# Four second-quarter f-tiles as seven-product blocks, with the sums that feed the down projection rearranged around them

## The chip, the cores and the metric

The kernel runs on one core of a Trainium2 chip. The metric is the device time of one launch in microseconds (us). The median before was 258.68 us in three runs (258.34 to 258.99), and 258.51 in four runs once the changed kernel was timed beside it. Most executions lie within 0.3% of the median, which is 0.8 us here. A verdict of faster or slower needs 2%.

Names: PE is TensorE's matmuls, PEld its weight loads, DVE is VectorE, ACT is ScalarE, POOL is GpSimd, and SPq is SyncE's queue, which issues most of the DMAs.

## The reference

```python
x = A_x                                            # 1 x 2048 x 640, bf16
g = sigmoid((x * gate_w).sum(-1, keepdims=True))
a = linear_attention(x, wqkv, H=32) @ wo           # phi(q), phi(k), kv and z per head
b = (gelu(x @ w_gate) * (x @ w_up)) @ w_down       # F = 1728 = 13 * 128 + 64
return g * a + (1 - g) * b
```

The attention output joins the down projection: its q rows, divided by their denominators, and a matrix M = kv @ wo are appended to h and w_down as further contraction rows.

## The kernel before: the parts that matter

The 2048 tokens are worked in four quarters of 512. For each quarter, stage E makes the h rows: for each f-tile of 128 rows it computes gate and up products, a gelu on ScalarE, and one product on VectorE that writes the row (`e_out`). Stage F is the down projection. The order is E(0), all q and k, the kv product, then E(1) F(0) E(2) F(1) E(3) F(2) F(3).

A plain f-tile is ten matmuls of 128x512:

```python
def phase_E(q, ft):                                         # cut
    psg = ps_tile(); e_mm(psg, wg, ft, q)        # 5 x (128x512)
    psu = ps_tile(); e_mm(psu, wu, ft, q)        # 5 x (128x512)
    e_out(q, ft, psg, psu)                       # gelu on ACT, product on DVE
```

A block makes the same f-tile by the Strassen-Winograd scheme: seven products of halves where the plain tile needs eight. It needs sums of weights (`sw_`, made once in the first quarter and stored in HBM), sums of tokens (`tx`), and sums of PSUM banks on the way:

```python
def unit_b(q, ft, fetch):
    ...
    def p5(): two(ub[:, hi_h], s_(1), tx[0], True)          # two(): 2 matmuls of 128x256
    def p1():
        two(ub[:, lo_h], wg[:, 0:2, fs], X[:, 0:2, lo_h])
        nc.scalar.copy(out=gb[:, lo_h], in_=ub[:, lo_h])
        nc.scalar.copy(out=cp, in_=ub[:, hi_h])
    def p6():
        two(ub[:, lo_h], s_(2), tx[1])
        nc.vector.tensor_tensor(out=gb[:, hi_h], in0=ub[:, lo_h], in1=cp, op=ALU.add)
    def p7(): ...                                           # 2 matmuls, an ACT copy
    def p3():
        nc.vector.tensor_tensor(out=ub[:, hi_h], in0=ub[:, hi_h], in1=c3, op=ALU.add)
        ...                                                 # 2 matmuls, read of a later block's sums
    def g5(): mm(gb, wg[:, 4, fs], X[:, 4, :])              # 128x512
    ...                                                     # p2: gelu; u5: 128x512; p4: e_out
    return [p5, p1], [p6], [p7, p3, g5, p2], [u5, p4]       # interleaved with three neighbours
```

Quarters 0, 2 and 3 use blocks. Quarter 1 does not:

```python
runs = {0: blocks([3], 12, range(4, 12), [NF - 1]),
        1: list(range(1, NF)),                              # plain tiles
        2: blocks([NF - 1, 12], 0, range(1, 12), [None]), ...}
```

Stage F uses the same scheme with S sums (of h and q rows) and T sums (of w_down and M), four each, in parts "h" (six k-tiles), "p" (two) and "x" (one). It works in two halves, `a`. All S and T sums of the first F were made on VectorE, nearly all of them during E(1), by the table `side`, which lists what is issued beside each step:

```python
side = {(1, 4): [(s3_tile,), (h_twin, 0), (phase_T, "h", (1,))],
        (1, 5): [(phase_T, "h", (3, 2))],
        (1, 6): [(phase_S, 0, "h", None, (3, 4)), (phase_T, "x", (1, 3))],
        ...                                                 # T p, S p, S x, more of T
        ("F", 0, 0): [(x_tiles,), (t_sums, 2), ...],        # token sums of quarter 2
        ("D", 0, 0): [(den_inv, 4), (den_mul, 6, 7)], ...}

def phase_F(q):                                             # cut
    for a in range(2):
        beside("F", q, a)
        x = ps_tile()                    # 2nd half: x's bank is b11's of the first half
        product(x, ...);  flush()        # flush: matmuls left over from E's last block
        beside("C", q, a)
        product(b11, ...)                # 9 matmuls of 128x320 each
        product(x, S2, T2); product(b22, S1, T1); join(d, b22)
        beside("D", q, a)
        product(x, S3, T3); product(b12, S4, ...)
        halves(...); join(o[0], b11)     # not a: this join reads b11's bank out
        join(o[0], b12); join(o[1], b22)
        product(b21, ..., T4); join(o[1], b21)
```

`join` is VectorE. `t_sums` makes the four token sums of a quarter, `den_mul`, `den_sum`, `den_rec`, `den_inv2` and `den_out` divide the q rows (POOL, DVE, POOL, DVE, POOL), and `pool_hold` copies one element on GpSimd to make that engine wait for a tile. Of the other names in these tables, those ending in `tiles` or `tile` only set up buffers, `h_twin` copies the last, half f-tile, `m_part` makes parts of M, and `w_fetch` reads weight sums from HBM.

## Time and profile before

| | before |
|---|---|
| time, median | 258.51 us |
| span of the profiled run | 256.9 us |
| PE busy | 251.3 us (98%) |
| E(1), counted from the kv product, and the first F | 29.52 + 17.87 = 47.39 us |

From the page of the kernel before, parts 1 and 4: busy us and share of the span of each engine with its number of instructions, then the chain of work that ended last, by engine.

```profile
PE 251.3 (98%) x1725; PEld 161.3 (63%) x1746; DVE 178.4 (69%) x343; ACT 118.8 (46%) x271; POOL 132.8 (52%) x154
PE 98%; issue 0%; DVE 0%
```

TensorE is the limit, and nothing else is on the chain. The next view is the busy time by stretches, E(1) from the kv product on and then the first F. Columns: the stretch, its length, then busy time and number of instructions for each engine, the granted clock, DMA share and GB/s.

```profile
core 0: us, PE busy (x) PEld busy (x) DVE busy (x) ACT busy (x) POOL busy (x), PEclk, DMA share, GB/s
98.07:127.59 29.52, 29.36 (x202) 13.76 (x205) 24.35 (x41) 12.44 (x27) 12.57 (x12) 1.00 0.34 99
127.59:145.46 17.87, 17.87 (x135) 12.55 (x134) 13.61 (x26) 4.37 (x8) 11.65 (x13) 1.00 0.29 82
```

PE has no gap in F and next to none in E; the clock is full. VectorE is 82% busy in E without being on the chain. I count E from the kv product because the first f-tile's first matmul has no record in several traces.

PE's timeline of the kernel before, around the first F's second half. Columns: start, busy us, engine, line, operation, output<-inputs, shapes, count, and in brackets idle time and what ended it, where PE waited.

```profile
135.67 0.99 PE L811 MATMUL banks<-hb,hT_148 128*128 128x320 f16 x6
136.50 0.57 PE L811 MATMUL banks<-hb,pqT_1266 128*128 128x320 f16 x3
136.90 0.98 PE L811 MATMUL banks<-wd,hT_148 128*128 128x320 bf16 x6
```

Read starts, not durations. Three 128x320 matmuls are shown as 0.57 us, but the next group starts 0.40 us later, because matmuls overlap. From start to start a 128x320 matmul takes 0.136 us and a 128x512 one 0.216. The line at 136.90 is the first product of the second half, and its bank was freed in time by VectorE (timeline of VectorE, kernel before):

```profile
135.53 0.55 DVE L713 RECIPROCAL rg<-dtmp 128x64 f32<-128x64 f32 x1 [0.42 <-POOL dtmp L706]
136.00 0.45 DVE L837 SCALAR_TENSOR_TENSOR o_out<-banks,omg_s,sw 128x320 bf16<-128x320 f32 x1
```

The join ends at 136.45, 0.45 us before PE uses the bank.

Blocks already run in the third quarter. Two lines of PE's timeline there, kernel before, are the same step of two successive blocks:

```profile
156.53 0.60 PE L316 MATMUL banks<-xT_90,wg 128*128 128x512 bf16 x3
158.49 0.60 PE L316 MATMUL banks<-xT_90,wg 128*128 128x512 bf16 x3
```

A block takes 1.96 us. A plain tile takes 10 x 0.216 = 2.16 us.

### The profile page before, as it was taken

How to read it: one execution, taken by the hardware profiler on the slowest of the kernel's cores; microseconds unless marked ns; L12 is line 12 of the kernel's file. 1: busy time of each engine (PE TensorE's matmuls, PEld its weight loads, DVE VectorE, ACT ScalarE, POOL GpSimd, SP SyncE). 2: the span in 40 equal slices, each digit the busy share in tenths (PEclk: the TensorE clock that was granted, in tenths of full speed). 3: DMA queues.
4: the chain of work that ended last, by engine and by line, in shares of the span. 5: the costliest groups of instructions: out<-in, count | busy, mean ns of one | idle time of the engine just before them, and what ended most of it. 6: DMA issues, size and time to landing. Idle time of an engine off the chain costs nothing.

```text
span 256.9 us, 4833 instructions
## 1 busy us (share of the span) xinstructions
PE 251.3 (98%) x1725; PEld 161.3 (63%) x1746; DVE 178.4 (69%) x343; ACT 118.8 (46%) x271; POOL 132.8 (52%) x154
## 2 busy tenths in 40 slices
PE   8999999999999999999999999999999999999994
PEld 3555786555556775444476668777666786767672
DVE  0567577788779997679997448884655887278632
ACT  2387676655554234732231168862126875311110
POOL 5005999355540003770048898992879999600000
PEclk9999999999999999999999999999999999999999
DMA  7999999500000019115031554442105710211011
GB/s 223 306 342 350 378 337 312 226 3 0 0 1 3 1 44 310 57 60 121 2 125 51 100 177 144 123 148 51 54 20 125 209 47 0 46 58 56 0 51 51
DMA packets 36361, 30.26 MB, mean 118 GB/s; under 512 B 13938, under 2 KB 34546, under 8 KB 36338
## 3 DMA queue, kind: packets, MB, share of 16 engines
q1 hardware_dynamic: 35618, 29.24, 37.5%
q10 hardware_dynamic: 720, 0.72, 0.9%
q8 instruction: 13, 0.21, 0.4%
q14 instruction: 10, 0.08, 0.1%
HBM read 21.01 MB, written 5.51 MB: 103 GB/s over the span
## 4 chain that ended last, share of the span: by engine, by line
PE 98%; issue 0%; DVE 0%
PE banks L811 27%; PE banks L316 23%; PE banks L406 17%; PE banks L228 14%; PE banks L326 6%; PE banks L528 6%; PE banks L518 2%; PE banks L203 1%; PE banks L818 1%; PE banks L659 0%; PE banks L628 0%; DVE o_out L837 0%; PE banks L598 0%
## 5 line engine op out<-in xcount | busy, mean ns | idle before, releaser
L233 ACT ACTIVATE gl<-banks 128x512 bf16<-128x512 f32 x52 | 31.0, 599 | 28.4 <-PE banks L228 17.1
L425 ACT ACTIVATE phi<-banks 128x512 bf16<-128x512 f32 (+1 forms) x36 | 18.7, 526 | 15.4 <-POOL hold L783 6.8
L238 DVE SCALAR_TENSOR_TENSOR hT_148<-banks,gl 128x512 bf16<-128x512 f32 x26 | 17.9, 691 | 9.0 <-PE banks L316 5.2
L238 DVE SCALAR_TENSOR_TENSOR hb<-banks,gl 128x512 bf16<-128x512 f32 x26 | 17.7, 682 | 8.5 <-PE banks L316 2.6
L833 ACT ACTIVATE m_all<-banks,omg_s 128x320 f32<-128x320 f32 x16 | 8.4, 527 | 31.6 <-PE banks L811 31.6
L783 POOL CAST hold<-phi 128x1 f32<-128x1 bf16 x13 | 2.4, 183 | 38.1 <-DVE phi L427 20.2
L316 PEld LDWEIGHTS <-wg 128*128 128x128 bf16 x150 | 14.7, 98 | 5.5
L380 DVE TENSOR_TENSOR banks<-banks,zacc 128x256 f32<-128x256 f32 x30 | 12.8, 427 | 6.0 <-ACT zacc L377 4.6
L228 PE MATMUL banks<-xT_89,wu 128*128 128x512 bf16 x63 | 16.0, 379 | 0.1
L837 DVE SCALAR_TENSOR_TENSOR o_out<-banks,omg_s,m_all 128x320 bf16<-128x320 f32 x24 | 12.4, 546 | 5.2 <-PE banks L811 5.2
L228 PE MATMUL banks<-xT_89,wg 128*128 128x512 bf16 x63 | 15.7, 379 | 0.1
L837 DVE SCALAR_TENSOR_TENSOR m_all<-banks,omg_s,m_all 128x320 f32<-128x320 f32 x8 | 4.4, 550 | 15.2 <-PE banks L811 15.1
L377 ACT COPY zacc<-banks 128x256 f32<-128x256 f32 x30 | 11.1, 371 | 7.1 <-PE banks L316 7.1
L316 PE MATMUL banks<-tx,wr 128*128 128x256 f16 x76 | 14.0, 273 | 0.0
L228 PEld LDWEIGHTS <-wu 128*128 128x128 bf16 x80 | 7.8, 98 | 9.4 <-DMA wu<-in_B_w_up_dram 0.3
L833 ACT ACTIVATE sw<-banks,omg_s 128x320 f32<-128x320 f32 x8 | 4.2, 527 | 19.6 <-PE banks L811 19.6
L228 PEld LDWEIGHTS <-wg 128*128 128x128 bf16 x80 | 7.5, 98 | 8.6 <-issue 0.5
L406 PE MATMUL banks<-wqk,xT_88 128*128 128x512 bf16 (+2 forms) x78 | 12.7, 321 | 0.1
L691 POOL TENSOR_TENSOR prod<-pq_92,zrep 128x640 f32<-128x640 bf16 x2 | 2.8, 1406 | 18.6 <-DVE kvt L635 18.6
L368 ACT COPY banks<-banks 128x256 f32<-128x256 f32 x30 | 10.7, 357 | 3.0 <-PE banks L316 0.4
L316 PEld LDWEIGHTS <-wu 128*128 128x128 bf16 x90 | 8.8, 98 | 4.6
L406 PE MATMUL banks<-wqk,xT_89 128*128 128x512 bf16 (+1 forms) x59 | 11.6, 343 | 0.1
(282 smaller groups left out, 671.1 us busy)
## 6 DMA issues: line engine op xcount, KB each, us to landing
wr<-stash SPq DMA_DIRECT2D x24, 128.0 KB, 2.2
x_all<-in_A_x_dram SPq DMA_DIRECT2D x4, 640.0 KB, 11.1
out_dram<-o_out SPq DMA_DIRECT2D x15, 160.0 KB, 1.9
wd<-in_B_w_down_dram SPq DMA_DIRECT2D x1, 2080.0 KB, 10.6
wr_1668<-stash SPq DMA_DIRECT2D x16, 128.0 KB, 2.5
wqk<-in_A_wqkv_dram SPq DMA_DIRECT2D x1, 800.0 KB
wg<-in_B_w_gate_dram SPq DMA_DIRECT2D x1, 800.0 KB
wu<-in_B_w_up_dram SPq DMA_DIRECT2D x1, 800.0 KB
```

The source lines that it names most:

```text
L228: nc.tensor.matmul(ps[:, t0 : t0 + tw], lhsT=w[:, dk, ft * P : (ft + 1) * P], rhs=xT[q][:, dk, t0 : t0 + tw], start=(dk == 0), stop=(dk == ...
L233: nc.scalar.activation(out=gl[:], in_=psg[:], func=ACT.Gelu_apprx_tanh)
L238: nc.vector.scalar_tensor_tensor(out=hT_cur[q][:, ft, :], in0=psu[:], scalar=HS, in1=gl[:], op0=ALU.mult, op1=ALU.mult)
L316: nc.tensor.matmul(out, lhsT=lhsT, rhs=rhs, start=start, stop=True, skip_group_check=True)
L326: return lambda: nc.tensor.matmul(ps, lhsT=w[:, k, f * P : (f + 1) * P], rhs=xT[q][:, k, :], start=(k == 0), stop=(k == ND - 1))
L380: nc.vector.tensor_tensor(out=ub[:, hi_h], in0=ub[:, hi_h], in1=c3, op=ALU.add)
L406: nc.tensor.matmul(ps[:, 0 : hi - lo], lhsT=xT[q][:, dk, sl * P : (sl + 1) * P], rhs=wqk[:, dk, lo:hi], start=(dk == 0), stop=(dk == ND - 1),)
L425: nc.scalar.activation(out=e[:, lo:top], in_=ps[:, lo:top], func=ACT.Exp)
L528: nc.tensor.matmul(bank[:, 0:HALF], lhsT=lhsT, rhs=rhs, start=(start and n == 0), stop=(stop and n == NG2 - 1), skip_group_check=True)
L811: nc.tensor.matmul(bank[:, 0:HALF], lhsT=lhs(sa, ia, ka * KS + kk, a), rhs=rhs(sb, kb * KS + kk, jb), start=(start and kk == 0), stop=(sto ...
L833: nc.scalar.activation(out=c[:], in_=bank[:, 0:HALF], func=ACT.Copy, scale=omg[i])
L837: nc.vector.scalar_tensor_tensor(out=out, in0=bank[:, 0:HALF], scalar=omg[i], in1=c[:], op0=ALU.mult, op1=ALU.add)
```

## The change

The intent is to give the second quarter four blocks (f-tiles 8 to 11). Their weight sums are read from HBM into h rows that are written only later and into the S4 tile. Their token sums lie where T4 will be. So S4 and T4, and for VectorE's sake also the third and fourth sums of p and x, move into the first F, and the first and second sums of p and x go to GpSimd. The read of w_down is split in two, so T sums can start earlier. The diff, cut to its core:

```diff
-    def x_tiles():
+    def x_tiles(tx=None):
...
+    WB = range(8, 12)
     runs = {
-        1: list(range(1, NF)),
+        1: blocks([7], 12, WB, [NF - 1]),
...
+    def early_blocks():                  # weight sums into h rows 8..11 and into S4's tile
+        rows = [hb[:, f * QW : (f + 2) * QW].bitcast(FP16) for f in (8, 10)]
+        rows += [SS["4"].rearrange("p k n -> p (k n)")[:, i * WS * P : (i + 1) * WS * P] for i in range(2)]
+        for ft, row in zip(WB, rows):
+            dma(out=row, in_=stash[WF.index(ft)])
...
-        (1, 1): [(m_part, 0), (t_tiles,), (den_mul, 0, 1, 2, 3)],
-        ...                              # S and T sums of (1, 4) to (1, 10), all on VectorE
+        ("S", 0): [(s_tiles, 0), (phase_S, 0, "h", None, (1,)), (x_early,), (t_sums, 1)],
+        ("P", 1): [(m_part, 0), (t_tiles,), (den_mul, 0), (phase_T, "h", (1,)), (hold, lambda: TS[1]),
+                   (den_mul, 1, 2), (den_sum, 0, 0)],
+        ...
+        ("P", 3): [(den_sum, 2, 0), (den_out, 0), (den_sum, 2, 1), (den_rec, 2), (phase_T, "h", (2,)),
+                   (hold, lambda: TS[2]), (den_out, 1), (den_inv2, 2)],
+        ("P", 4): [(s3_tile,), (h_twin, 0)],
+        ("P", 5): [(phase_S, 0, "h", None, (3,)), (hold, lambda: SS[0, 3]), (den_out, 2, 3)],
+        ("P", 6): [(den_mul, 4, 5)] + [(phase_T, part, which, nc.gpsimd) ...]       # p, x: 1, 2
+        + [(phase_S, 0, part, None, (1, 2), nc.gpsimd) for part in "px"],
+        ("C", 0, 0): [(phase_T, "p", (3,)), (phase_T, "x", (3,)), (phase_S, 0, "p", None, (3, 4)),
+                      (phase_S, 0, "x", None, (3, 4)), (phase_S, 0, "h", None, (4,))]
+        + [(phase_T, part, (4,)) for part in "hpx"],
+        ("D", 0, 0): [(t_sums, 2), (lambda: pool_hold(ew["tx"][3][:, 0, 0:1]),), (den_mul, 6, 7), (den_inv2, 4)],
...
+        early_blocks()
+        for ft in range(1, WB[0] - 1):   # f-tiles 1 to 6 stay plain, with fixed banks for 5 and 6
+            if ft > WB[0] - 4:
+                bank_at[0] = 6 if ft == WB[0] - 3 else 4
+            phase_E(1, ft)
+            beside("P", ft)
```

More of the change, by code (lines that the diff above doesn't have):

```diff
@@ L129 @@
     ew = {}
-    def x_tiles():
-        tx = big.tile([P, 10 * HT], FP16, name="tx", tag="pq", bufs=NQ)
+    def x_tiles(tx=None):
+        tx = big.tile([P, 10 * HT], FP16, name="tx", tag="pq", bufs=NQ) if tx is None else tx
         ew["tx"] = [tx[:, 2 * HT * n : 2 * HT * (n + 1)].rearrange("p (k c) -> p k c", k=2) for n in range(4)]
@@ L194, in load_down @@
         wd = ov.tile([P, NF, D], BF16, name="wd", tag="slab_d")
-        dma(out=wd[:, 0 : NF - 1, :], in_=B_w_down[0:FM, :].rearrange("(k p) n -> p k n", p=P))
+        wd_v = B_w_down[0:FM, :].rearrange("(k p) n -> p k n", p=P)
+        for lo, hi in ((0, KH), (KH, NF - 1)):
+            dma(out=wd[:, lo:hi, :], in_=wd_v[:, lo:hi, :])
         for lo in (0, FL):
@@ L748, in ktile, with phase_T @@
         return ktiles(part, k, first, second)[:, kk - PART[part][0], :]
-    def phase_T(part, which=(1, 2, 3, 4)):
+    def phase_T(part, which=(1, 2, 3, 4), eng=nc.vector):
         lo, hi = PART[part]
@@ L758, in phase_T @@
             a0, a1 = {1: ((0, 1), (0, 0)), 2: ((1, 1), 1), 3: ((1, 1), (0, 1)), 4: ((1, 0), 2)}[i]
-            sums(t[i], blk(*a0), blk(*a1) if i in (1, 3) else t[a1], ALU.subtract)
+            sums(t[i], blk(*a0), blk(*a1) if i in (1, 3) else t[a1], ALU.subtract, eng)
     SS = {}
@@ L906, in run_E @@
     def run_E(q):
-        if q == 1:
-            for n, ft in enumerate(runs[q]):
-                phase_E(q, ft)
-                beside(q, n + 1)
-            return
         pipe, plain, at = [], {}, []
@@ L988, with x_early @@
     TS[4] = hb[:, NF * QW : NF * QW + KS * HALF].bitcast(FP16).rearrange("p (k n) -> p k n", n=HALF)
+    def x_early():
+        x_tiles(hb[:, NF * QW : NF * QW + 10 * HT].bitcast(FP16))
+    def early_blocks():
+        rows = [hb[:, f * QW : (f + 2) * QW].bitcast(FP16) for f in (8, 10)]
+        rows += [SS["4"].rearrange("p k n -> p (k n)")[:, i * WS * P : (i + 1) * WS * P] for i in range(2)]
+        for ft, row in zip(WB, rows):
+            row = row.rearrange("p (s c) -> p s c", c=P)
+            dma(out=row, in_=stash[WF.index(ft)])
+            ew["at"][1, ft] = split(row)
     hT_cur[2] = hT0
@@ L1014, in m_part, with hold @@
         phase_M(((0, 0), (0, 1), (1, 0)) if i == 0 else ((1, 1), (2, 0), (2, 1)))
+    def hold(of):
+        pool_hold(of()[:, 0, 0:1])
     def s_pool(q, a, parts="hpx"):
@@ L1019 @@
     side.update({
-        ("S", 0): [(s_tiles, 0), (phase_S, 0, "h", None, (1,))],
-        ("S", 1): [(phase_S, 0, "h", None, (2,))],
-        (1, 1): [(m_part, 0), (t_tiles,), (den_mul, 0, 1, 2, 3)],
-        (1, 2): [(m_part, 1), (den_inv, 0), (den_out, 0, 1)],
-        (1, 3): [(den_inv, 2), (den_out, 2, 3)],
-        (1, 4): [(s3_tile,), (h_twin, 0), (phase_T, "h", (1,))],
-        (1, 5): [(phase_T, "h", (3, 2))],
-        (1, 6): [(phase_S, 0, "h", None, (3, 4)), (phase_T, "x", (1, 3))],
@@ L1028 @@
-        (1, 7): [(phase_T, "h", (4,)), (phase_T, "x", (2, 4))],
-        (1, 8): [(phase_T, "p", (1, 2, 3, 4))],
-        (1, 9): [(phase_S, 0, "p")],
-        (1, 10): [(phase_S, 0, "x")],
-        (1, 12): [(lambda: pool_hold(SS[0, 4][:, KS - 1, 0:1]),), (den_mul, 4, 5)],
-        ("F", 0, 0): [(x_tiles,), (t_sums, 2), (w_fetch, (2, 1), (2, 2), (2, 3))],
-        ("D", 0, 0): [(den_inv, 4), (den_mul, 6, 7)],
-        ("F", 0, 1): [(h_twin, 1), (den_sum, 6, 0), (den_sum, 6, 1), (den_rec, 6), (den_out, 4, 5)],
+        ("S", 0): [(s_tiles, 0), (phase_S, 0, "h", None, (1,)), (x_early,), (t_sums, 1)],
@@ new lines @@
+        ("P", 0): [(phase_S, 0, "h", None, (2,)), (hold, lambda: SS[0, 2])],
+        ("P", 1): [(m_part, 0), (t_tiles,), (den_mul, 0), (phase_T, "h", (1,)), (hold, lambda: TS[1]),
+                   (den_mul, 1, 2), (den_sum, 0, 0)],
+        ("P", 2): [(m_part, 1), (den_sum, 0, 1), (den_rec, 0), (phase_T, "h", (3,)), (hold, lambda: TS[3]),
+                   (den_mul, 3), (den_inv2, 0)],
+        ("P", 3): [(den_sum, 2, 0), (den_out, 0), (den_sum, 2, 1), (den_rec, 2), (phase_T, "h", (2,)),
+                   (hold, lambda: TS[2]), (den_out, 1), (den_inv2, 2)],
@@ new lines @@
+        ("P", 4): [(s3_tile,), (h_twin, 0)],
+        ("P", 5): [(phase_S, 0, "h", None, (3,)), (hold, lambda: SS[0, 3]), (den_out, 2, 3)],
+        ("P", 6): [(den_mul, 4, 5)] + [(phase_T, part, which, nc.gpsimd) for part, which in (("p", (1, 2)), ("x", (1, 2)))]
+        + [(phase_S, 0, part, None, (1, 2), nc.gpsimd) for part in "px"],
+        (1, 6): [(den_rec, 4)],
+        ("F", 0, 0): [(x_tiles,), (w_fetch, (2, 1), (2, 2), (2, 3))],
+        ("C", 0, 0): [(phase_T, "p", (3,)), (phase_T, "x", (3,)), (phase_S, 0, "p", None, (3, 4)),
+                      (phase_S, 0, "x", None, (3, 4)), (phase_S, 0, "h", None, (4,))]
@@ L1036 @@
+        + [(phase_T, part, (4,)) for part in "hpx"],
+        ("D", 0, 0): [(t_sums, 2), (lambda: pool_hold(ew["tx"][3][:, 0, 0:1]),), (den_mul, 6, 7), (den_inv2, 4)],
+        ("F", 0, 1): [(h_twin, 1), (den_out, 4, 5), (den_sum, 6, 0), (den_sum, 6, 1), (den_rec, 6)],
         ("D", 0, 1): [(den_inv2, 6), (den_out, 6, 7)],
@@ L1055 @@
     })
-    for q, st in ((2, 8), (3, 14)):
+    for q, st in ((1, 4), (2, 8), (3, 14)):
         for n in range(4):
-            side[q, 3 + n] = [(den_sum, st, n // 2, slice(H // 2 * (n % 2), H // 2 * (n % 2 + 1)))]
+            side[q, (3 if q > 1 else 2) + n] = [(den_sum, st, n // 2, slice(H // 2 * (n % 2), H // 2 * (n % 2 + 1)))]
     with tc.manual_schedule():
@@ L1064 @@
         phase_KV()
+        early_blocks()
         phase_Zrep()
+        beside("P", 0)
+        for ft in range(1, WB[0] - 1):
[3 more added lines that the diff above has]
+            beside("P", ft)
         for q in range(1, NQ):
```

## The prediction

> **What bounds it now.** TensorE. The page gives PE 251.3 us busy of a 256.9 us span (98%); the chain of waits is PE for 98% of it. The table by stretches gives PE 21.48 of 21.59 us in the plain f-tiles of the second quarter (104.9 to 126.5) and 18.95 of 18.95 in the first F (126.5 to 145.5). No gap there can be won; only fewer streamed columns shorten it. VectorE has 19.64 and 14.69 us in these stretches: off the chain, with little room.
>
> **On PE.** A plain f-tile is ten 128x512 matmuls; in the timeline it repeats every 2.16 us. A seven-product block is fourteen 128x256 and two 128x512: 4608 columns for 5120. In the third quarter, where blocks already run, it repeats every 1.96 us. That is 0.20 us a tile, not 10% (0.216): the six more matmuls cost a little each. The Trainium skill ("TensorE: Matmul & The Clock Gate", "Wait — 56ns, not 53.3ns?") gives about 2.5 ns per matmul beyond its columns; the trace agrees (14 x 109 + 2 x 216 ns = 1.96 us). Four tiles: 0.79 us, all on the chain.
>
> **Added and moved elsewhere.**
> - ScalarE: 12 copies of 0.36 to 0.38 us; it was busy 8.4 of 21.6 us there, so free.
> - VectorE: 8 sums of banks (0.42 us); 4 token sums (0.42 us) earlier. To make room, T and S sums of "p" and "x" (first, second) go to GpSimd; the third and fourth, with S4 and T4 of the h rows, go into the first F. Blocks with a den sum beside them fill VectorE about 1.8 of 1.96 us in the third quarter without a PE gap, so I expect none here.
> - Large T sums: the first took 1.90 us and the third 1.62 beside GpSimd work, the second and fourth 1.14 alone. The skill ("GPSIMD Engine Reference", "1. Specifications") says the two engines share SBUF interfaces; the trace agrees in kind. The new holds keep GpSimd out: these should drop to 1.2 to 1.5.
> - DMA: four 256 KB reads around 100 us, needed at about 116. Free.
>
> **Where some is lost.** In the first F, VectorE gets about 4.4 us of moved sums after the last delayed h row, then the join of d, four token sums (1.58 us), a reciprocal, and only then the join that frees bank 11, which the second half's first product reuses. From the trace's starts I put that join's end about 9.9 us after F begins; PE wants the bank at about 9.75 (9.31 in the old F plus 0.43 of delayed matmuls). Before, the join ended 0.45 us early. I expect a PE gap of about 0.2 us (0 to 0.5). The third and fourth products' operands should be about 1 us early.
>
> **Sum.** -0.79 + 0.2 = -0.6 us: 258.1 us, range 257.5 to 258.9. Faster by over 2%: 0.005; within 2%: 0.985; slower by over 2%: 0.01.
>
> **What would show it.** Right: 24 more matmuls; the second quarter's E about 0.75 us shorter and gapless; later stages equal, shifted; one short PE wait on VectorE at the first product of F's second half; first T sum well under 1.9 us. Wrong: PE gaps between blocks released by VectorE or ScalarE (sums late behind den sums that wait for GpSimd); an F gap over 0.5 us, or at the third product; F waiting for GpSimd's S2 or T2.
>
> **What would make it wrong.** VectorE over half a microsecond late anywhere in those 30 us; GpSimd late with S2/T2 (I put it 1.5 us early); or no F gap, giving 257.9.

## The result, and the profile after

| | before | after |
|---|---|---|
| time, median (range) | 258.51 us (258.31 to 258.99) | 258.34 us (258.18 to 258.69) |
| ratio | | 0.9993, 95% interval 0.9974 to 1.0011 |
| span of the profiled run | 256.9 us | 256.4 us |
| E(1) from the kv product | 29.52 us | 28.68 us |
| first F | 17.87 us | 18.72 us |
| both | 47.39 us | 47.41 us |

A ratio is the mean time of one kernel's fast runs over that of the other's fast runs of the same rounds, so it is not quite the ratio of the medians.

Stages are counted from start to start of matmuls. "First F" includes 0.43 us of matmuls that the last block leaves to F; plain tiles leave none. Without these, E fell by 0.84 - 0.43 = 0.41 us and F grew by 0.85 - 0.43 = 0.42, so the blocks' gain is gone by the time the third quarter starts. The spans differ by 0.5 us for other reasons: the changed kernel's trace reaches the kv product 0.26 us sooner and has 0.5 us less behind its last matmul, and a wait in the fourth quarter, below, takes 0.29. Such things vary: in the second trace of the kernel before the kv product starts at 97.79 us, in the first at 98.07, and in a later run's trace (e4_plain_moves) at 99.60, where PE waits 1.6 us for one of the first weight loads from HBM.

Page of the changed kernel, parts 1 and 4:

```profile
PE 251.9 (98%) x1770; PEld 163.5 (64%) x1770; DVE 178.9 (70%) x349; ACT 122.8 (48%) x283; POOL 143.0 (56%) x167
PE 93%; DVE 3%; DMA 1%; issue 1%; DVEq 0%
```

There are 24 more weight loads (1770 for 1746), as six more matmuls in four blocks need. DVE now has 3% of the chain. The stretches, changed kernel:

```profile
97.81:126.49 28.68, 28.45 (x226) 15.81 (x226) 22.78 (x38) 16.47 (x40) 21.98 (x24) 1.00 0.46 137
126.49:145.21 18.72, 18.52 (x139) 12.84 (x137) 15.38 (x34) 4.14 (x8) 12.35 (x15) 1.00 0.28 78
```

GpSimd went from 12.57 to 21.98 us in E. VectorE is no busier over the two stretches (38.16 us for 37.96), yet PE now waits for it. The waits of PE, changed kernel, with total us, times, and longest:

```profile
PE banks L318 <- DVE hb L240: 0.2, 1, 0.2
PE banks L813 <- DVE o_out L839: 0.2, 1, 0.2
```

Both are larger than these totals say. PE's timeline at the first one:

```profile
113.30 1.24 PE L328 MATMUL banks<-xT_89,wg 128*128 128x512 bf16 x5
114.77 0.38 PE L318 MATMUL banks<-hb 128*128 128x256 f16 x2 [0.23 <-DVE hb L240]
```

Five matmuls from 113.30 on leave PE free for the next at 113.30 + 5 x 0.216 = 114.38. It starts at 114.77, so 0.39 us are lost. The brackets count from the modelled end of the last matmul and miss 0.16 us of it. The line at 114.77 is the first product of the first block, and VectorE's timeline shows what it waits for:

```profile
111.22 1.24 DVE L61 TENSOR_TENSOR t_1223<-wd,t_1090 128x1920 f16<-128x1920 bf16 x1
113.03 0.55 DVE L715 RECIPROCAL rg<-dtmp 128x64 f32<-128x64 f32 x1 [0.58 <-POOL dtmp L708]
113.50 1.22 DVE L240 SCALAR_TENSOR_TENSOR hb<-banks,gl 128x512 bf16<-128x512 f32 x2
114.64 0.95 DVE L61 TENSOR_TENSOR sw<-hT_148 128x1536 f16<-128x1536 bf16 x1
```

VectorE runs its queue in order. A reciprocal sits there waiting 0.58 us for two small GpSimd operations, and behind it are the h rows of f-tiles 4 and 5 (113.50, two of them). PE had gone on from f-tile 4 to the next at 108.98 and from f-tile 5 at 111.14, and their gelus ended on ScalarE at 108.70 and 110.86, so both had been ready for about 4 and 2 us when the reciprocal began at 113.03. The second row ends at 114.72 and frees the bank that the block's first product takes. GpSimd's timeline shows why the reciprocal was late:

```profile
111.54 1.46 POOL L708 TENSOR_SCALAR dtmp<-den,en_s 128x32 f32<-128x32 f32 x2
113.05 0.18 POOL L785 CAST hold<-t_1223 128x1 f32<-128x1 f16 x1
```

The two small operations take 1.46 us while VectorE makes the second T sum (111.22 to 112.46). In the kernel before the same two took 0.67 us at 110.37, while VectorE was idle.

The second wait, in PE's timeline of the changed kernel:

```profile
135.06 0.99 PE L813 MATMUL banks<-hb,hT_148 128*128 128x320 f16 x6
135.88 0.57 PE L813 MATMUL banks<-hb,pqT_1298 128*128 128x320 f16 x3
136.66 0.98 PE L813 MATMUL banks<-wd,hT_148 128*128 128x320 bf16 x6 [0.20 <-DVE o_out L839]
```

PE could start at 135.88 + 3 x 0.136 = 136.29 and starts at 136.66, so 0.37 us are lost. VectorE's timeline before that:

```profile
134.24 0.41 DVE L61 TENSOR_TENSOR tx<-xT_90 128x512 f16<-128x512 bf16 x1
134.68 0.42 DVE L61 TENSOR_TENSOR tx<-xT_90,tx 128x512 f16<-128x512 bf16 x1
135.02 0.42 DVE L61 TENSOR_TENSOR tx<-xT_90 128x512 f16<-128x512 bf16 x1
135.36 0.42 DVE L61 TENSOR_TENSOR tx<-xT_90,tx 128x512 f16<-128x512 bf16 x1
135.69 0.54 DVE L715 RECIPROCAL rg<-dtmp 128x64 f32<-128x64 f32 x1
136.16 0.45 DVE L839 SCALAR_TENSOR_TENSOR o_out<-banks,omg_s,sw 128x320 bf16<-128x320 f32 x1
```

The join of b11 now ends at 136.61, after the moved sums, the token sums and the reciprocal, where it ended 0.45 us early before.

### The profile page after: what moved, and what is told of

It is laid out like the page before. It is cut to its first block, busy times and chain, and to the rows that moved or that the text cites. A ratio compares the mean times of both kernels' runs of the same rounds, so it can differ in the third digit from the quotient of the medians.

```text
span 256.4 us, 4953 instructions
## 1 busy us (share of the span) xinstructions
PE 251.9 (98%) x1770; PEld 163.5 (64%) x1770; DVE 178.9 (70%) x349; ACT 122.8 (48%) x283; POOL 143.0 (56%) x167
## 4 chain that ended last, share of the span: by engine, by line
PE 93%; DVE 3%; DMA 1%; issue 1%; DVEq 0%
PE banks L318 25%; PE banks L813 24%; PE banks L408 17%; PE banks L230 9%; PE banks L328 8%; PE banks L530 6%; PE banks L520 2%; DMA wr<-stash 1%; PE banks L205 1%; PE banks L820 1%; DVE sp L61 1%; DVE tx L61 0%; PE banks L661 0%; PE banks L630 0%; DVE o_out L839 0%
## 5 line engine op out<-in xcount | busy, mean ns | idle before, releaser
L318 PEld LDWEIGHTS <-wg 128*128 128x128 bf16 x170 | 16.6, 98 | 6.4
L382 DVE TENSOR_TENSOR banks<-banks,zacc 128x256 f32<-128x256 f32 x34 | 14.5, 427 | 7.2 <-ACT zacc L379 5.7
L379 ACT COPY zacc<-banks 128x256 f32<-128x256 f32 x34 | 12.6, 370 | 8.1 <-PE banks L318 8.1
L370 ACT COPY banks<-banks 128x256 f32<-128x256 f32 x34 | 12.1, 357 | 3.2 <-PE banks L318 0.3
L318 PEld LDWEIGHTS <-wu 128*128 128x128 bf16 x102 | 10.0, 98 | 5.2
L701 DVE TENSOR_REDUCE den<-prod 128x16 f32<-128x320 f32 (+1 forms) x20 | 12.0, 609 | 0.5 <-POOL prod L693 0.4
L408 PE MATMUL banks<-wqk,xT_89 128*128 128x512 bf16 (+1 forms) x60 | 11.6, 344 | 0.0
L408 PE MATMUL banks<-wqk,xT_90 128*128 128x512 bf16 (+1 forms) x60 | 11.5, 344 | 0.0
L408 PE MATMUL banks<-wqk,xT_91 128*128 128x512 bf16 (+1 forms) x60 | 11.5, 344 | 0.0
L318 PE MATMUL banks<-tx,wu 128*128 128x256 f16 x60 | 11.5, 273 | 0.0
```

The source lines that it names most:

```text
L318: nc.tensor.matmul(out, lhsT=lhsT, rhs=rhs, start=start, stop=True, skip_group_check=True)
L408: nc.tensor.matmul(ps[:, 0 : hi - lo], lhsT=xT[q][:, dk, sl * P : (sl + 1) * P], rhs=wqk[:, dk, lo:hi], start=(dk == 0), stop=(dk == ND - 1),)
```

## The experiments

Theory: four blocks save 0.79 us of PE time, and two waits of PE on VectorE, 0.39 us before the first block and 0.37 us in the first F, give nearly all of it back. Rivals: the block is worth less here than in the third quarter; a true gain of 0.6 us is hidden in the noise of whole times (rival 1 below); the waits have other causes (rival 2), or a full VectorE only moves them elsewhere (rival 3). The eleven runs were all correct and all profiled runs but one fast; the repeat of the kernel before was a single look, whose state is unknown, and only its trace is used.

| run | E | first F | both | fourth quarter's E | median | ratio to before (95%) |
|---|---|---|---|---|---|---|
| before, two traces | 29.52 | 17.87 | 47.39 | 26.52 | 258.5 to 258.7 | 1 |
| after | 28.68 | 18.72 | 47.41 | 26.81 | 258.34 | 0.9993 (0.9974 to 1.0011) |
| after_again | 28.69 | 18.72 | 47.41 | 26.67 | 258.88 | 1.0000 (0.9987 to 1.0014) |
| e1_tokens_late | 28.69 | 18.36 | 47.04 | 26.52 | 258.11 | 0.9974 (0.9960 to 0.9988) |
| e2_rec_late | 28.29 | 18.69 | 46.98 | 26.80 | 258.39 | 0.9979 (0.9963 to 0.9994) |
| e3_both | 28.29 | 18.36 | 46.65 | 26.82 | 257.93 | 0.9968 (0.9953 to 0.9982) |
| e3_again | 28.29 | 18.36 | 46.65 | 26.89 | 257.99 | 0.9972 (0.9957 to 0.9986) |
| e4_plain_moves | 29.52 | 17.87 | 47.39 | 26.52 | 258.30 | 0.9993 (0.9962 to 1.0024) |
| e5_sums_vector | 29.02 | 20.20 | 49.22 | 26.52 | 260.29 | 1.0055 (1.0028 to 1.0082) |
| e6_two_more_sums | 28.68 | 19.64 | 48.32 | 26.52 | 259.40 | 1.0023 (0.9996 to 1.0051) |
| e8_turn_late | 28.29 | 18.36 | 46.65 | 26.52 | 257.66 | 0.9957 (0.9936 to 0.9978) |
| e8_again | 28.29 | 18.36 | 46.65 | 26.52 | 257.67 | 0.9971 (0.9952 to 0.9990) |

Stages are in us, counted in each run's trace as above (differences of printed starts can be 0.01 off); "before" is the median of the kernel before in the rounds of each call (258.51, 258.69, 258.74, 258.63).

### after_again and before_again: the two kernels once more

No edit. Changed kernel:

> The changed kernel once more. My theory (two waits of TensorE on VectorE eat the gain of the blocks): the two gaps are in this trace too, at the first block's first product (0.39 us from start to start more than the columns need) and at the first product of the first F's second half (0.37 us); the stretch from the second quarter's first matmul to the third quarter's is again 49.6 to 49.7 us, as in the kernel before (49.64). The wait on a weight-sum read in the fourth quarter (0.28 us in the first trace) is chance and need not return. Rival 1 (the small gain measured is only noise about a true gain of 0.6 us): the stretch is about 49.0 us here. Time ratio to the kernel before by my theory 0.998 to 1.001.

Kernel before:

> The kernel before, for a second trace. Counted from the kv product: E plus F 47.39 us as in the first trace, so that differences of 0.02 us between traces mean little. Fourth quarter: 26.52 us if the wait on a weight-sum read comes from the change, 26.5 to 26.8 if it is chance.

Stages repeat to 0.02 us in both kernels: 47.41 again after, 47.39 again before. The time ratio came out as 1.000. So a gain of 0.6 us hidden by noise is ruled out; in this stretch the change gains nothing. In this trace the profile puts the first wait down to a DMA, yet PE's start lies just behind the same VectorE row as before, and e2 below settles which it is.

### e1_tokens_late: token sums behind the joins

```diff
-  ("D", 0, 0): [(t_sums, 2), (lambda: pool_hold(ew["tx"][3][:, 0, 0:1]),), (den_mul, 6, 7), (den_inv2, 4)],
-  ("F", 0, 1): [(h_twin, 1), ...
+  ("D", 0, 0): [(lambda: pool_hold(TS[4][:, KS - 1, 0:1]),), (den_mul, 6, 7), (den_inv2, 4)],
+  ("F", 0, 1): [(t_sums, 2), (h_twin, 1), ...
```

GpSimd's hold waited for the last token sum, so it moves too, to the last T4 sum.

> The four token sums of the third quarter go behind the joins of the first F's first half on VectorE, so the join that frees the reused bank comes about 1.5 us earlier. My theory: the gap of 0.37 us in F goes away, the first F is 18.35 us for 18.72, the E part of the second quarter stays at 30.9 us with its 0.39 us gap; 0.37 us faster than the changed kernel. Rival 2 (the product waits for something else, such as the copy of the x bank or a transpose, and VectorE is only the last seen): the gap stays at 0.2 us or more, released by another engine.

F fell to 18.36 us and its gap is gone; E kept its own at 28.69. Rival 2 is out for the F gap: the product waited for VectorE's late join. The fourth quarter's wait was absent in this trace. The whole time fell by 0.26% against the kernel before.

### e2_rec_late: the reciprocal behind an h row

```diff
-  (hold, lambda: TS[2]), (den_out, 1), (den_inv2, 2)],
-  ("P", 4): [(s3_tile,), (h_twin, 0)],
+  (hold, lambda: TS[2]), (den_out, 1)],
+  ("P", 4): [(s3_tile,), (h_twin, 0), (den_inv2, 2)],
```

> The second reciprocal, which waits 0.58 us for GpSimd in VectorE's queue ahead of two h rows, goes behind the first of these rows. My theory: the h row that frees the first block's bank ends about 0.6 us earlier, the gap of 0.39 us before the first block goes away, the E part is 30.55 us for 30.93, the F part stays at 18.7 us with its gap; 0.39 us faster than the changed kernel. Rival (the blocks themselves start late, from weight sums read from memory or from the token sums): the gap stays, with another releaser.

E is 28.29 us, 0.39 less, with no PE gap left in it; F kept its gap (18.69). So the first wait came from the order in VectorE's queue, and not from late weight sums, token sums or DMAs. The expected 30.55 and 30.93 us count from the first f-tile, the other figures from the kv product 2.25 us later; the difference of 0.39 is the same.

### e3_both and e3_again: both moves

The edits of e1 and e2 together.

> Both moves at once. My theory: the gains add, as each gap is on TensorE's chain: the stretch of E and F is 48.9 us for 49.65, all of the 0.79 us that four blocks save shows, and the time is 0.7 to 0.8 us under the kernel before, ratio about 0.997, beating both kernels. Rival 3 (taking one wait away only lets TensorE arrive earlier at a next wait on VectorE, which is nearly full): the stretch is 49.2 us or more, with a new gap released by VectorE.

> The run with both moves once more, beside the next on the same chip. E plus F again 46.65 us; ratio to before 0.996 to 0.998. If the wait in the fourth quarter is chance, this trace may be without it.

The gains add: E plus F is 46.65 us, 0.76 under the changed kernel and 0.74 under the kernel before. The expected 48.9 us counts from the first f-tile; less 2.25 us it is 46.65. Rival 3 is out: no new gap appeared. PE's timeline at the first block and at F's second half, run e3_both:

```profile
113.99 1.24 PE L328 MATMUL banks<-xT,wg 128*128 128x512 bf16 x5
115.07 0.38 PE L318 MATMUL banks<-hb 128*128 128x256 f16 x2
...
136.18 0.57 PE L813 MATMUL banks<-hb,pqT 128*128 128x320 f16 x3
136.59 0.98 PE L813 MATMUL banks<-wd,hT 128*128 128x320 bf16 x6
```

From start to start these are 1.08 and 0.41 us: no gap. VectorE's timeline at the first block, same run:

```profile
113.08 0.68 DVE L240 SCALAR_TENSOR_TENSOR hb<-banks,gl 128x512 bf16<-128x512 f32 x1
113.73 0.55 DVE L715 RECIPROCAL rg<-dtmp 128x64 f32<-128x64 f32 x1
114.20 0.63 DVE L240 SCALAR_TENSOR_TENSOR hb<-banks,gl 128x512 bf16<-128x512 f32 x1
```

The first h row takes the place in which VectorE had stood idle, and the reciprocal no longer waits. The second row ends at 114.83, before PE wants the bank at 115.07. Both runs are faster than the kernel before in their intervals (0.9953 to 0.9982 and 0.9957 to 0.9986), by far less than 2%. The changed kernel, run in the same rounds as e3_both (after_again), had 0.9987 to 1.0014, so e3_both is faster than that too.

### e4_plain_moves: the moved sums without blocks

Tiles 7 to 13 of the second quarter are plain again, with the same `side` lists; no early token sums and no early reads of weight sums. The fixed banks of f-tiles 5 and 6 go too.

```diff
-            run_E(q)
+            if q == 1:
+                for n, ft in enumerate(range(WB[0] - 1, NF)):
+                    phase_E(1, ft)
+                    beside(1, n)
+            else:
+                run_E(q)
```

> Only the moved sums, no blocks: all f-tiles of the second quarter are plain again, without early token sums and reads of weight sums. My theory: counted from the first product after the middle stage (the kv product), E is 29.52 us as before, so the blocks alone are what takes E to 29.52 - 0.79 = 28.73 less nothing; the first F has no delayed rows ahead of the moved sums, so VectorE starts them about 1.3 us earlier and F is 17.9 to 18.1 us for the 17.87 of before (18.73 - 0.43 delayed = 18.30 with the gap in the changed kernel). Ratio to before 1.000 to 1.001. Rival (the moved sums by themselves make F too long for VectorE): F is 18.2 us or more here too.

Both stages are as in the kernel before (29.52 and 17.87 us): with plain tiles the moves cost nothing, so that rival is out. Against e3_both, where E plus F is gapless too, four blocks are worth 47.39 - 46.65 = 0.74 us here, or 0.80 in E (29.52 - 28.29 - 0.43) less 0.05 in F, to rounding. The block is worth what the third quarter said.

This run also shows what the first wait needs. VectorE's and PE's timelines of e4_plain_moves:

```profile
114.48 0.55 DVE L715 RECIPROCAL rg<-dtmp 128x64 f32<-128x64 f32 x1 [0.58 <-POOL dtmp L708]
114.95 1.22 DVE L240 SCALAR_TENSOR_TENSOR hb<-banks,gl 128x512 bf16<-128x512 f32 x2
...
115.09 1.24 PE L230 MATMUL banks<-xT,wg 128*128 128x512 bf16 x5
116.17 1.24 PE L230 MATMUL banks<-xT,wu 128*128 128x512 bf16 x5
```

The reciprocal waits for GpSimd ahead of the same two rows as in the changed kernel, and the second row ends at 116.17. Yet no matmul starts late: the groups of five keep their 1.08 us. So the order in VectorE's queue costs PE time only where a product soon wants the bank that the second row frees, as the first block's first product does. Whether another choice of banks would have avoided the wait was not tried.

### e5_sums_vector: sums back on VectorE

```diff
-  ("P", 6): [(den_mul, 4, 5)] + [(phase_T, part, which, nc.gpsimd) for part, which in (("p", (1, 2)), ("x", (1, 2)))]
-  + [(phase_S, 0, part, None, (1, 2), nc.gpsimd) for part in "px"],
+  ("P", 6): [(den_mul, 4, 5)],
...
+  side[1, 3].append((phase_T, "p", (1, 2)))
+  side[1, 4] += [(phase_T, "x", (1, 2)), (phase_S, 0, "p", None, (1,))]
+  side[1, 5] += [(phase_S, 0, "p", None, (2,)), (phase_S, 0, "x", None, (1, 2))]
```

> The changed kernel with the first and second T and S sums of p and x back on VectorE, spread beside the blocks, and not on GpSimd. They cost about 2.4 us there; VectorE idles about 1.3 us between the second block and F in the changed kernel. If the move to GpSimd is needed, VectorE falls 1 us or more behind: E plus F, counted from the kv product, is 48.0 to 48.9 us for 47.41, with most of the loss at the first product of F's second half. If the move was not needed, 47.4 to 47.6.

It is slower than expected, 49.22 us. PE's waits on VectorE in this run:

```profile
PE banks L820 <- DVE m_all L839: 0.5, 1, 0.5
PE banks L318 <- DVE banks L382: 0.4, 1, 0.4
PE banks L813 <- DVE o_out L839: 0.4, 1, 0.4
PE banks L318 <- DVE hb L240: 0.2, 1, 0.2
PE banks L318 <- DVE banks L375: 0.2, 1, 0.2
```

I had expected most of the loss in one place. A VectorE that is behind delays PE wherever a bank passes between them: between blocks, at the left-over matmuls, at the halves, and at F's second half. So the move of these sums to GpSimd is needed with this schedule, or other places for them on VectorE, which no run tried.

### e6_two_more_sums: a dose

```diff
-  ("D", 0, 0): [(t_sums, 2), (lambda: pool_hold(...
+  ("D", 0, 0): [(t_sums, 2), *2 * [(lambda: sums(ew["tx"][3], xT[2][:, 2:4, 0:HT], ew["tx"][1], ALU.subtract),)],
+                (lambda: pool_hold(...
```

> The changed kernel with the fourth token sum made three times over, ahead of the join that frees the reused bank. Dose test of the F gap: each repeat is 0.34 us from start to start, so the gap grows from 0.37 to about 1.05 us and F from 18.73 to 19.4 us; E stays at 28.68. If the product waits for something else, F stays at 18.7 to 18.9.

F grew to 19.64 us, by 0.92 for two repeats where I expected 0.68. The repeats take 0.46 us each from start to start in VectorE's timeline (all three 1.33 us), not 0.34; the result is unchanged. What VectorE does ahead of that join is paid in full by PE.

### e8_turn_late and e8_again: transposes out of the way of reads

e3_both, and two transposes of q rows go from the fourth quarter's start into the third F:

```diff
-  (3, 0): [(s_tiles, 2), (den_inv2, 12), (den_out, 12, 13), *s_pool(2, 0)],
+  (3, 0): [(s_tiles, 2), (den_inv2, 12), (lambda: den_out(12, 13, later=True),), *s_pool(2, 0)],
-  ("F", 2, 0): [(den_turn, 14, 15)],
+  ("F", 2, 0): [(den_turn, 12, 13, 14, 15)],
```

> Both moves of the earlier run, and the two transposes of q rows that stand in the DMA queue ahead of the fourth quarter's weight-sum reads go behind them, into the third F. My theory: E and F of the second quarter stay at 46.65 us; the wait of TensorE on a read in the fourth quarter (0.3 us in three of five traces of changed kernels, absent in one and in the kernel before) cannot occur, so that quarter is 26.52 us for 26.82; from the kv product to the last matmul 154.3 us for 155.10 before; ratio to before 0.996 to 0.997. If the wait comes from the reads themselves, 26.7 to 26.8 stays.

> Both moves and the late transposes once more. E plus F 46.65 us, fourth quarter 26.52 us again, ratio 0.0005 to 0.001 under that of both moves if the wait that it removes happens in about half of the executions; no difference if the wait is rare.

It tests the wait of the fourth quarter. In five of nine traces of kernels made from the change that keep these transposes in place, PE waits 0.15 to 0.37 us in the fourth quarter, and in four of the five the chain of waits names a read of weight sums. It was absent in both traces of the kernel before, and in both of e8. That is no proof that the transposes cause it: four of the nine traces with them in place are without it too, and e8 has only two. e8 is the shortest version in the traces: from the kv product to the last matmul 154.29 us, for 155.10 before and 155.34 after. In whole times e8 (0.9957 and 0.9971) cannot be told from e3 (0.9968 and 0.9972), and the expected difference of 0.0005 to 0.001 between e8_again and e3_again, timed in the same rounds, did not show (0.9971 for 0.9972). Why the wait shows up in some traces and not in others, and whether the change as such makes it likelier, stays open.

## Why the prediction was right or wrong

The time, 258.1 us with 257.5 to 258.9, holds the 258.34 measured. The range holds the time of the kernel before (258.51) as well. The gain of 0.6 us was not there: E plus F went from 47.39 to 47.41 us. Point by point:

- **"Four tiles: 0.79 us, all on the chain": right.** Plain tiles with the same moves against blocks without gaps (e4, e3) give 0.80 us in E. The count of matmuls and their spacing was enough.
- **"Blocks with a den sum beside them fill VectorE about 1.8 of 1.96 us ... so I expect none here": the step that failed.** Between blocks there is indeed no gap. There is one of 0.39 us ahead of the first block, and e2 shows it came from the order in VectorE's queue, a reciprocal waiting for GpSimd with two ready h rows behind it. I judged VectorE by its load in the steady state, read from another quarter, and not by who stands behind whom where the blocks start. The prediction did list VectorE work late behind operations that wait for GpSimd as a sign of being wrong, but looked for it between blocks. e4 adds that the same stall costs nothing with plain tiles. The Trainium skill ("TensorE: Matmul & The Clock Gate", the table of specifications at its head) calls VectorE's queue a strict FIFO; the trace agrees, as rows that had been ready for 2 to 4 us did not pass the waiting reciprocal.
- **"I expect a PE gap of about 0.2 us (0 to 0.5)" in F: right place and cause, mis-sized.** It measured 0.37 us. I put the join's end 9.9 us after F begins and it was 136.61 - 126.49 = 10.12; the bank was wanted 9.80 us after, for my 9.75. The cause is shown by e1 (gone) and e6 (grows with the dose). e4 shows what the moved sums need to hurt: without blocks, VectorE gets to them 1.80 us after F begins (130.92 - 129.12) and not 2.94 (129.43 - 126.49), and they cost nothing.
- **The sum:** 0.79 - 0.39 - 0.37 leaves 0.03 us, against 0.02 lost as measured. The term for E that was taken as zero is most of the miss; the rest is the F term, 0.37 for 0.2.
- **"The new holds keep GpSimd out: these should drop to 1.2 to 1.5": wrong, but for the direction of the first.** The first T sum fell from 1.90 to 1.54 us, the third stayed at 1.61 (1.62 before), and the second rose from 1.14 to 1.24. A hold stops what comes behind it in GpSimd's queue. It does not stop what already runs: at the third sum GpSimd still had a product and the two small operations ahead of its hold.
- **GpSimd in time with S2 and T2: right.** Its last S2 sum, of the x part, ended at 129.33 us, and PE did not wait for GpSimd in F. The product that reads it begins at 129.42 and takes the x part last, so by an estimate from the spacing of 0.136 us it was wanted at 130.51: 1.2 us early, for 1.5 predicted.
- **"The third and fourth products' operands should be about 1 us early": right**, about 0.8 and 0.9 us: S3 complete at 131.08 for 131.87, S4 at 132.15 for 133.09.
- **"Later stages equal, shifted": not in all.** The changed kernel's trace has a wait of 0.29 us in the fourth quarter that the kernel before's has not.

## What to carry to other kernels

When a change on a full engine shortens it by tenths of a microsecond, go through the queue of every in-order engine that hands it buffers, item by item, at the places where the pattern changes: an average load with room to spare says nothing about a ready item behind a waiting one. A stall on such an engine costs time only where the full engine soon needs what stands behind it (e4). Put operations that wait for a third engine behind work that is already due, and work that is needed late behind work that frees a buffer; here two such moves on VectorE turned a null result into all of the 0.74 us that the blocks were worth. Measure such effects by stages from start to start in the trace, which repeated to 0.02 us, while whole times varied by over 1 us.

## What the Trainium skill lacked or had wrong

- "TensorE: Matmul & The Clock Gate", "Back-to-back issue gap": it gives about 131 ns per matmul as the sustained spacing at 512 columns in a stream of weight loads and matmuls, and says that columns over 2.4 GHz plus 2.5 ns over-counts there. Here every matmul has its own weight load, and the sustained spacing is 216 ns at 512 columns and 109 ns at 256, which is the formula that the page calls isolated.
- "GPSIMD Engine Reference", "1. Specifications": it says that GpSimd and VectorE contend for SBUF interfaces and gives no size, and no page was found that has one for these operations. Here a 128x512 token sum takes 0.42 us in the changed kernel and 1.35 and 1.38 us in e3_both beside GpSimd products (timeline of VectorE from 137.26 us); two 128x32 operations on GpSimd take 0.67 us, and 1.46 us beside a VectorE sum of two SBUF tiles. Both engines lose.
- "Perfetto Trace Analysis", "Per-engine timelines": it calls the end time of a matmul a model and not a measurement, but does not say that the idle time before the next matmul then understates the loss. Here the profile showed 0.23 and 0.20 us where 0.39 and 0.37 were lost from start to start, and removing the waits gave back 0.39 and 0.36.
